# Eight PE tiles at a time for the backward 32x32 products, and 32x32 transpositions of pairs of bf16 as 4-byte elements

## The chip, the cores and the metric

One core of one Trainium2 chip. The metric is the device time of one execution in microseconds; the time before is the median of three runs. A profile is one execution, taken by the hardware profiler. In it PE is the matmul engine, PEld its weight loads, DVE the vector engine, ACT the scalar engine, POOL and SP the two engines that start most of the DMAs. L399 is line 399 of the kernel before.

## The reference

A forward pass and its gradient, on 2048 rows of 512 bf16 values. The forward pass is a layer norm, then the sum of a recurrent attention and a dense branch. What matters here is the attention: 32 heads of 128, the sequence cut into 64 segments of 32 rows, and a memory of 8 rows that each segment hands to the next.

```python
for s in range(n_seg):                                   # 64, in order
    h = jnp.concatenate([mem, xs], axis=1)               # 8 + 32 rows
    q, k, v = (jnp.einsum('btd,dhe->bhte', h, W) for W in (Wq, Wk, Wv))
    scores = jnp.where(mask, jnp.einsum('bhqe,bhke->bhqk', q, k) * scale, -1e9)
    p = softmax(scores)
    o = jnp.einsum('bhqk,bhke->bhqe', p, v)              # per head: 40x40 by 40x128
    o = jnp.einsum('bhte,hed->btd', o, Wo)
    mem = o[:, :M]
    outs.append(o[:, M:])
```

The backward pass runs the segments from the last to the first. Per head it needs dV = P^T dO, dP = dO V^T, dS from dP and P, dK = dS^T Q and dQ = dS K, then the gradient of h from dQ, dK, dV by Wq, Wk, Wv, whose first 8 rows are handed to the segment before. The gradients of the weights are summed over all rows. Eleven outputs in all.

## The kernel before, in words

The rows of a segment are kept as 32 "A" rows (8 of memory, the last 24 of the segment) that lie on the recurrence, and the first 8 rows of four segments are gathered into one "L" block of 32 rows (16 blocks in all). The L blocks hang on the recurrence only through what they share with it, and their work is used as filler. Everything is therefore 32 rows high, and a tile of 128 partitions by 8 x 128 holds 32 heads: partition 32j + r is row r, column block i is head 4i + j (j from 0 to 3, i from 0 to 7). This is the layout of qN, kN, vN, oN, gN, dN and dLN ("NAT"). The transposed layout "TR" ([128 elements of a head, i, j, 32 rows]) serves as weights (lhsT) of the PE.

Stages, each with its own planner: the dense branch with layer norm; the forward chain of 64 segments (`chain`, with `l_proj` and `l_attn` for the L blocks and `dw_unit`, the dense branch's weight gradients, as filler); turning Wv, Wk, Wq and Wo into the layouts of the backward pass (`turn`, `turn_o`); the backward chain of 64 segments (the second `chain`, with `load`, `l_pre` and `l_post`); the weight gradients of the attention (L1497 on).

Order of work: each stage adds its operations to a `_Plan` with an estimated cost per engine, the keys it reads and writes, and a priority. `run` (L101) computes ranks and writes out one fixed order; each engine then runs its own instructions in that order, and waits where a result is not there yet. PSUM has eight banks. `Stage.bank` (L350) hands them out by turn from rings per kind of use ("c" for the chain, "f" for filler, "r" for a long sum), in the order in which the program adds the operations, and the order of the plan follows from it.

One backward segment (L1300 to L1363): `proj` computes gO (32 matmuls of 32 columns of weights by 512, four column strips of the array at once, two halves), `to_T_plain` transposes it on the PE, two half runs compute dP, four DVE steps (`smax_bwd`, L1165 to L1170) give dS. `part` (L1319) is called for dV (2), dK (1) and dQ (0): `diag` (L441) multiplies per head, `sq_T` (L395) transposes the result in 32x32 blocks on DVE into dT, `dh_part` (L1174) multiplies dT by the turned weights into one long sum, dRA. Its result R_A is copied out (L1339), a small product (gm, L1349) takes the rows of the memory, and a copy (L1353) puts them into the next gO's input. So dRA, R_A, gm, gO, dP and dS form the recurrence.

`diag` computes a half (4 of the 8 column blocks i) in one PSUM bank: for each i and each of two terms, four products of 32x32 weights by 32x128, one for each j, at tile (32j, 32j) of the array: rows 32j on, columns 32j on. Four products are under way at once, on the diagonal. Its result is copied to bf16 by ACT or DVE (`evict`). The forward pass uses `diag` for O (L992 and L938), the backward for dV, dK, dQ (L1320) and dqL (L1222); `l_post` writes the same form by hand (own, L1254), and adds products of the full 128 rows to it (mm, L1265) from the loads xs and ys; dLN is stored to S_GNL and, for its first part, read back.

`sq_T`: for a half, one DVE instruction transposes 512 columns of bf16, as 16 blocks of 32x32 per strip of 32 partitions; the elements of a head are taken with a step of four (e = 4a + c), so that partition 32j + a of the result holds elements 4a + c of head 4i + j. The weights of the following product (Wo by `wo_part`, L854; turned Wq, Wk, Wv by `wtf`) are laid out to match.

## Time and profile before

| what | value |
|---|---|
| runs, us | 3017.47, 3035.89, 3026.65; median 3026.65 |
| span of the profiled execution, us | 3018.8 |
| PE, PEld, DVE, ACT, POOL busy, us | 2761.1, 1575.5, 1551.3, 967.4, 372.8 |
| DMA moved | 590 MB, 195 GB/s on average |
| mean granted clock of the PE | 0.976 |

The execution whose span this is ran its instructions over 3018.8 us; the times of the runs have the start and end of an execution around the span. Times inside the profile count from the start of the span. The stages lie at about 0 to 236 (dense branch), 236 to 1240 (forward chain), 1240 to 1276 (turning), 1276 to 2440 (backward chain), 2440 to 2490 (loads before the weight gradients) and 2490 to 3018.

```profile
PE 2761.1 (91%) x59680; PEld 1575.5 (52%) x59680; DVE 1551.3 (51%) x3367; ACT 967.4 (32%) x2013; POOL 372.8 (12%) x640
```

A group's line gives the line of the kernel, the engine, the operation, what it writes and reads, its shapes and count, then its busy time, the mean of one in ns, and the engine's idle time just before it with what ended that. "128*32 128x512" on a matmul is a weight of 128 rows by 32 columns and a moving operand of 128 by 512. A matmul's duration includes its way through the array, so many overlap; how fast they follow each other is read from the starts, in the view in order of time.

### The profile page before, as it was taken

How to read it: one execution, taken by the hardware profiler on the slowest of the kernel's cores; microseconds unless marked ns; L12 is line 12 of the kernel's file. 1: busy time of each engine (PE TensorE's matmuls, PEld its weight loads, DVE VectorE, ACT ScalarE, POOL GpSimd, SP SyncE). 2: the span in 40 equal slices, each digit the busy share in tenths (PEclk: the TensorE clock that was granted, in tenths of full speed). 3: DMA queues.
4: the chain of work that ended last, by engine and by line, in shares of the span. 5: the costliest groups of instructions: out<-in, count | busy, mean ns of one | idle time of the engine just before them, and what ended most of it. 6: DMA issues, size and time to landing. Idle time of an engine off the chain costs nothing.

```text
span 3018.8 us, 132985 instructions
## 1 busy us (share of the span) xinstructions
PE 2761.1 (91%) x59680; PEld 1575.5 (52%) x59680; DVE 1551.3 (51%) x3367; ACT 967.4 (32%) x2013; POOL 372.8 (12%) x640
## 2 busy tenths in 40 slices
PE   8998899999999999888888888888889889999998
PEld 6664555555555555655454545454555444444444
DVE  5544555555555655666555555565556522232322
ACT  4324444444454444333333333333333310000000
POOL 1111111111111111100000000000000002111111
PEclk9999999999999999899999999999999999999999
DMA  6648655556555666457777877777777689788861
GB/s 202 221 141 227 166 170 168 162 159 172 167 166 162 174 182 179 135 162 197 196 208 197 211 215 208 202 204 207 204 215 205 193 292 311 232 262 271 248 182 42
DMA packets 543946, 590.15 MB, mean 195 GB/s; under 512 B 230342, under 2 KB 344183, under 8 KB 541199
## 3 DMA queue, kind: packets, MB, share of 16 engines
q1 hardware_dynamic: 527934, 527.05, 61.2%
q0 software_dynamic: 15440, 54.61, 5.4%
q8 instruction: 466, 7.63, 1.1%
q14 instruction: 106, 0.86, 0.1%
HBM read 283.32 MB, written 262.68 MB: 181 GB/s over the span
## 4 chain that ended last, share of the span: by engine, by line
PE 64%; issue 11%; DMA 10%; DVE 9%; SPq 2%; ACT 2%; POOL 1%; DVEq 0%; ACTq 0%; POOLq 0%
PE ps_gw L1517 11%; PE ps_dRA L1181 7%; PE ps_d L451 6%; PE ps_q L415 4%; PE ps_k L415 3%; PE ps_RA L863 3%; PE ps_h L622 3%; PE ps_gO L415 3%; PE ps_dw L1073 2%; PE ps_v L415 2%; PE ps_dRL L1181 2%; PE ps_B L650 2%; SPq L361 2%; PE ps_gxb L650 2%; DMA dLN<-S_GNL 1%
## 5 line engine op out<-in xcount | busy, mean ns | idle before, releaser
L1181 PE MATMUL ps_dRA<-WA,dT 128*32 128x512 bf16 x6144 | 382.5, 388 | 13.9 <-issue 10.2
L1517 PE MATMUL ps_gw<-WA,WB 128*128 128x512 bf16 x1536 | 332.3, 379 | 0.6 <-DVE gwo L316 0.6
L415 PEld LDWEIGHTS <-PA 128*32 128x32 bf16 x8192 | 204.9, 98 | 239.2 <-DVE PA L1011 27.0
L399 DVE STREAM_TRANSPOSE dT<-dN 128x512 bf16<-128x512 bf16 x384 | 255.6, 692 | 104.9 <-ACT dN L318 103.4
L1517 PEld LDWEIGHTS <-WB 128*128 128x128 bf16 x1896 | 185.4, 98 | 225.0 <-issue 1.7
L318 ACT CAST dN<-ps_d 128x512 bf16<-128x512 f32 x357 | 199.2, 588 | 287.5 <-PE ps_d L451 270.1
L1181 PEld LDWEIGHTS <-dT 128*32 128x32 bf16 x6144 | 158.5, 98 | 175.7 <-issue 34.4
L316 DVE CAST gwo<-ps_gw 128x512 bf16<-128x512 f32 x64 | 39.7, 683 | 401.7 <-PE ps_gw L1517 268.2
L318 ACT CAST gwo<-ps_gw 128x512 bf16<-128x512 f32 x64 | 32.9, 599 | 515.4 <-PE ps_gw L1517 357.9
L1291 POOL COPY bVT<-VR 128x1024 bf16<-128x1024 bf16 x64 | 66.7, 1043 | 965.9 <-PE ps_dP L1313 917.7
L415 PE MATMUL ps_q<-WA,PA 128*32 128x512 bf16 x2048 | 159.3, 387 | 8.4 <-DVE PA L1011 8.3
L316 DVE CAST kN<-ps_k 128x512 bf16<-128x512 f32 x120 | 83.0, 691 | 160.4 <-PE ps_k L415 158.7
L451 PEld LDWEIGHTS <-PB 32*32 32x32 bf16 x8192 | 119.1, 92 | 79.3 <-issue 45.9
L415 PE MATMUL ps_k<-WA,PA 128*32 128x512 bf16 x2048 | 158.0, 385 | 0.0
L415 PE MATMUL ps_gO<-WB,PA 128*32 128x512 bf16 x2048 | 138.3, 414 | 16.8 <-DVE PA L1353 15.3
L863 PE MATMUL ps_RA<-WB,OT 128*32 128x256 bf16 x4096 | 128.3, 275 | 14.6 <-DVE OT L399 10.5
L318 ACT CAST qN<-ps_q 128x512 bf16<-128x512 f32 x124 | 72.6, 586 | 198.8 <-PE ps_q L415 183.0
L1073 PE MATMUL ps_dw<-sx,anT 128*128 128x512 bf16 x448 | 123.7, 384 | 9.3 <-DMA sx<-in_grad_out_dram 4.7
L415 PE MATMUL ps_v<-WA,PA 128*32 128x512 bf16 x2048 | 129.3, 380 | 0.0
L863 PEld LDWEIGHTS <-OT 128*32 128x32 bf16 x4096 | 103.9, 97 | 39.1 <-DVE OT L399 30.6
L844 POOL TENSOR_TENSOR P<-P,rsA 128x320 bf16<-128x320 bf16 x64 | 46.2, 722 | 534.3 <-DVE rsA L839 228.1
L1181 PE MATMUL ps_dRL<-WA,LT 128*32 128x512 bf16 x1536 | 108.9, 387 | 2.3 <-issue 1.2
(307 smaller groups left out, 4920.1 us busy)
## 6 DMA issues: line engine op xcount, KB each, us to landing
S_GN<-dN SPq DMA_DIRECT2D x192, 256.0 KB
WA<-S_GN SPq DMA_DIRECT2D x160, 256.0 KB
S_Q<-qN SPq DMA_DIRECT2D x64, 256.0 KB
S_K<-kN SPq DMA_DIRECT2D x64, 256.0 KB
S_V<-vN SPq DMA_DIRECT2D x64, 256.0 KB
S_ON<-oN SPq DMA_DIRECT2D x64, 256.0 KB
bqN<-S_Q SPq DMA_DIRECT2D x64, 256.0 KB
bkN<-S_K SPq DMA_DIRECT2D x64, 256.0 KB
```

The costliest lines, as they stand in the source:

```text
L316: nc.vector.tensor_copy(out, in_)
L318: nc.scalar.copy(out, in_)
L399: self.plan.add({"DVE": 0.70}, lambda e, x=x: nc.vector.transpose(dst[:, x, :, :], src[:, x, :].rearrange("p i (a c) -> p i c a", c=JQ)), ...
L415: nc.tensor.matmul(bk()[32 * j:32 * (j + 1), :], lhsT=win(dc), rhs=Wt(dc, c0), start=(dc == 0), stop=(dc == DC - 1), tile_position=(0, 32 ...
L451: nc.tensor.matmul(bk()[32 * j:32 * j + m, k * P:(k + 1) * P], lhsT=lf(j, i), rhs=rf(j, i), start=(k == 0 and x == 0), stop=(x == n - 1), ...
L622: nc.tensor.matmul(bk()[:, x, :], lhsT=Wt[:, dc, fc * P:(fc + 1) * P], rhs=In[:, dc, :], start=(dc == 0), stop=(dc == DC - 1), skip_group_ ...
L650: nc.tensor.matmul(bk()[:], lhsT=src[z][:, fc, rc * P:(rc + 1) * P], rhs=Wt[:, fc, :], start=(fc == 0 and first), stop=(fc == FC - 1))
L863: nc.tensor.matmul(bk()[32 * c:32 * (c + 1), :], lhsT=OTt[:, i, j, :], rhs=Wo[:, JQ * i + j, dh * DH:(dh + 1) * DH], start=(i == 0 and j < ...
L1073: nc.tensor.matmul(bks[x]()[:], lhsT=anT[x][:, c, :], rhs=sx[z][:], start=(c == 0), stop=(c == TC - 1))
L1181: nc.tensor.matmul(bk()[32 * j:32 * (j + 1), :], lhsT=XT[:, i, j, :], rhs=wtf(t, JQ * i + j), start=(first and i == 0), stop=(last and i = ...
L1291: A({"POOL": 1.0}, lambda e: nc.gpsimd.tensor_copy(VT[:, :, :, M:KA].rearrange("p i j r -> p (i j) r"), VR[:].rearrange("p i j r -> p (i j ...
L1517: nc.tensor.matmul(bks[n]()[:], lhsT=HNc[:, rc, dc * P:(dc + 1) * P], rhs=gns[y][:, hf * 512:(hf + 1) * 512], start=(y == 0), stop=(y == N ...
```

## The change: what it does

Five things go together.

**1. The products.** `cross` takes the place of `diag` in the backward pass. A half is now two values of j with all eight i, in place of all j with four i. The product of strip j and column block i goes to tile (32j, 32c), where c = i % 4: the rows are still those of strip j, but the result lands in partitions 32c on. Four column strips times two row strips (y) are addressed one after the other, eight tiles, and each of the two row strips writes its own PSUM bank (columns 0 to 255 of it). The eviction reads both banks in one instruction of 512 elements.

```diff
+        def cross_mm(self, bk, half, terms, first):
+            for s_ in range(2):
+                for x, (lf, rf, m) in enumerate(terms):
+                    for y in range(2):
+                        j = 2 * half + y
+                        for c in range(JQ):
+                            i = JQ * s_ + c
+                            nc.tensor.matmul(
+                                bk()[32 * c:32 * c + m, y, s_ * P:(s_ + 1) * P], lhsT=lf(j, i), rhs=rf(j, i),
+                                start=(first and s_ == 0 and x == 0), stop=(x == len(terms) - 1),
+                                tile_position=(32 * j, 32 * c), skip_group_check=True,
+                            )
+
+        def cross_evict(self, half, bk, dst, prio):
+            self.evict(lambda: dst[1][:, 4 * half:4 * half + 4, :].rearrange("p (y s) e -> p y (s e)", y=2), bk,
+                       lambda: bk()[:, :, 0:2 * P], [(dst[0], half)], prio, EV_F)
...
-                sg.diag("c", "d%d" % t, terms, rk, ("dN%d" % t, dN[t]), 0)
+                sg.cross("d%d" % t, terms, rk, ("dN%d" % t, dN[t]), 0, LIFT[t])
...
-            sg.diag("f", "dqL", [
+            sg.cross("dqL", [
```

`cross` plans a half as 0.115 us a term (`diag`: 0.23), and lists the half of its destination among the keys that the product writes. `l_post` does the same by hand: its own product uses `cross_mm` and now lists the loads xs and ys among what it reads; the product of 128 rows keeps its 16 matmuls a half on four column strips and writes the same two banks.

**2. The transpositions.** `sq_T`, in both passes, moves 4-byte words: 256 a half instead of 512 elements, so the element of a head that lands on partition a is e = 4a + 2c + z, with z the place in the pair. The two values of a pair stay neighbours, so a weight of 32 columns is read with a step of two elements, by `rows`.

```diff
+            words = lambda t, x: t[:].rearrange("p i j r -> p (i j r)").bitcast(F32)[:, 2 * P * x:2 * P * (x + 1)]
             for half in range(2):
-                x = slice(4 * half, 4 * half + 4)
-                self.plan.add({"DVE": 0.70}, lambda e, x=x: nc.vector.transpose(
-                    dst[:, x, :, :], src[:, x, :].rearrange("p i (a c) -> p i c a", c=JQ)),
+                self.plan.add({"DVE": 0.43}, lambda e, half=half: nc.vector.transpose(
+                    words(dst, half).rearrange("p (i c r) -> p i c r", i=4, c=2),
+                    src[:].rearrange("p i e -> p (i e)").bitcast(F32)[:, 2 * P * half:2 * P * (half + 1)]
+                    .rearrange("p (i a c) -> p i c a", i=4, c=2)),
                     [(sk, half)], [(dk, half)], prio)
+
+        def rows(self, XT, i, q):
+            return XT[:].rearrange("p i (c z) r -> p i c (z r)", c=2)[:, i, q // 2].rearrange("p (r z) -> p z r", z=2)[:, q % 2]
...
-                            nc.tensor.matmul(bk()[32 * j:32 * (j + 1), :], lhsT=XT[:, i, j, :],
-                                             rhs=wtf(t, JQ * i + j), start=(first and i == 0),
+                            nc.tensor.matmul(bk()[32 * j:32 * (j + 1), :], lhsT=sg.rows(XT, i, j),
+                                             rhs=wtf(t, i, j), start=(first and i == 0),
...
-                                    bk()[32 * c:32 * (c + 1), :], lhsT=OTt[:, i, j, :],
+                                    bk()[32 * c:32 * (c + 1), :], lhsT=sg.rows(OTt, i, j),
```

**3. The order of heads.** Strip j, column block i now holds head 16(i // 4) + 4j + i % 4. The moving operand of `proj` (`wf`) becomes one run of 512, the loads of Wo, `turn`, `wtf` and the stores of the weight gradients follow the new order; in the weight gradients the moving operand of L1517 becomes four runs of 128.

```diff
     def wf(t):
-        w = Wqkv[t].rearrange("p c (i j e) -> p c i j e", i=NI, j=JQ)
-        return lambda dc, c0: w[:, dc, c0 % HW // P:c0 % HW // P + 4, c0 // HW, :]
+        w = Wqkv[t].rearrange("p c (s j f) -> p c s j f", s=2, j=JQ)
+        return lambda dc, c0: w[:, dc, c0 % HW // 512, c0 // HW, :]
...
-    def wtf(t, h):
+    def wtf(t, i, q):
+        h = 16 * (i % 2) + JQ * (i // 2) + q
         return Wqkv[t][:, :, h * P:(h + 1) * P]
```

**4. The banks.** In the backward stage a bank is no longer handed out by turn: the planner picks, when it places the first operation on a bank, the one that has been free longest among those that the kind may use, and a kind may hold only so many at once. An operation without a free bank waits its turn in the plan. The other stages keep their rings.

```diff
-        sg = Stage(plan, {"c": (pc, 5), "r": (pc, 1), "f": (pc, 2)})
+        S3 = [("c", x) for x in range(3)]
+        sg = Stage(plan, pc, {"c": (3, S3), "f": (1, S3), "w": (3, S3), "r": (1, [("r", 0)]), "d": (2, [("d", 0), ("d", 1)]),
+                              "t": (3, [("r", 0), ("d", 0), ("d", 1)])})
...
             for o in elig:
+                got = slots(o)
+                if got is None:
+                    continue
...
                     for d in o.deps:
                         t = max(t, d.end if d.eng == e and e != "SP" else d.end + d.lat + g)
+                    for x in got:
+                        t = max(t, x[0] + g)
```

"d" is a pair of banks, two of them; so the eight banks are three shared by chain and filler, one for dRA (and the last dRL), and two pairs. `turn` in the backward stage uses "t". The factor `ACCP` and the three values of `LIFT` that the planner can weigh in are zero.

**5. The weight gradients.** The eight banks of a group are now three of "w", the one of "r" and the two pairs of "d", each pair one tile. Before the stage, three instead of four banks take early products (`mm0`).

274 lines of the change are left out of this document (154 added, 120 removed).

## The prediction

> **What bounds the kernel now.** I read the busy times by stage first, cut where the lines change: the dense branch, the forward chain of 64 segments, the turning of the weights, the backward chain of 64 segments, the loads before the weight gradients, the weight gradients. Columns: PE, weight loads, DVE, ACT, POOL, then granted clock, DMA share and GB/s.
>
> ```profile
> 0.00:236.00 236.00, 222.52 (x1654) 149.52 (x1658) 125.93 (x498) 86.49 (x213) 36.31 (x85) 1.00 0.61 194
> 236.00:1240.00 1004.00, 928.36 (x23600) 552.46 (x23589) 571.44 (x1232) 457.02 (x1021) 142.18 (x263) 0.99 0.61 171
> 1276.00:2440.00 1164.00, 1018.71 (x31361) 594.32 (x31359) 678.95 (x1349) 377.18 (x694) 91.52 (x140) 0.96 0.73 202
> 2490.00:3018.00 528.00, 520.48 (x2411) 235.69 (x2409) 146.34 (x240) 32.86 (x64) 97.31 (x144) 1.00 0.71 222
> ```
>
> PE is busy 92% of the forward chain, 88% of the backward chain and 99% of the weight gradients; DVE is at 57% and 58% in the two chains. PE bounds all three, and the backward chain leaves it 145 us idle, 2.3 us of each segment's 18.2 us. So PE time removed there should show, and DVE time only where PE waits for it. Next, the groups and the order of time inside one backward segment:
>
> ```profile
> L399 DVE STREAM_TRANSPOSE dT<-dN 128x512 bf16<-128x512 bf16 x384 | 255.6, 692 | 104.9 <-ACT dN L318 103.4
> L399 DVE STREAM_TRANSPOSE OT<-oN 128x512 bf16<-128x512 bf16 x128 | 88.9, 705 | 20.0 <-ACT oN L466 15.9
> L1330 DVE STREAM_TRANSPOSE PB<-maskA 128x256 bf16<-128x256 bf16 x64 | 27.7, 433 | 0.0
> ```
>
> ```profile
> 1611.51 0.28 PE L1313 MATMUL ps_dP<-bVT,gOT 128*32 128x40 bf16 x16
> ...
> 1617.68 0.23 PE L451 MATMUL ps_d<-bkN,PB 32*32 32x128 bf16 x4
> 1617.75 0.22 PE L451 MATMUL ps_d<-bkLN,PB 32*32 32x128 bf16 x4
> ...
> 1618.53 0.22 PE L451 MATMUL ps_d<-bkLN,PB 32*32 32x128 bf16 x4
> 1618.68 3.64 PE L1181 MATMUL ps_dRA<-WA,dT 128*32 128x512 bf16 x64
> ```
>
> The 64 products of one gradient (both halves) go four at a time: the first four start at 1617.68, the sixteenth four at 1618.53, the next work at 1618.68. That is 0.85/15 = 56.7 ns for four, 14.2 ns for a product, 1.00 us for the whole.
>
> Last, the chain of waits over the backward stage: of its 1164 us, pieces named DMA add to 134 us and pieces of SP's queue to 21 us (the sum of the 200 longest), 13% together; "issue" is 11.7%. The longest are the dLN round trip and the xs and ys loads, some 5 us each.
>
> **PE: the 32x32 products.** Twice as many tiles work at once, with the same number of products and weight loads. No row shows eight tiles in two strips of rows. Upper end of the cost: nothing gained, 14.2 ns each. Lower end: the fastest pairs of weight load and product in this trace. ps_dP starts 16 in 0.28 - 0.18 us (its own product lasts 0.18), 6.7 ns each; ps_dPL (64 from 1283.58 to 1284.07) 7.7 ns. Eight in 56.7 ns would be 7.1 ns. I take 7.2 ns, the mean of the two rows: 64 x (14.2 - 7.2) = 0.45 us a run.
> - Backward chain: 3 gradients x 64 segments + 16 dqL = 208 runs, 208 x 0.45 = 93.6 us.
> - The own product of l_post: 2 parts x 16 blocks, 32 runs of 32 products, 0.22 us each, 7.0 us.
>
> Together 101 us of PE time. The forward products (L992, L938) still go through diag and gain nothing.
>
> How much of it passes to the end: the part of the stage's chain that isn't DMA or SP's queue is 87%; if the "issue" share doesn't shrink either it is 75%. I take 80%: **-80 us** (ends -101 and 0). The recurrence doesn't stop it earlier: from gO (1608.03) to dS (1614.69) is 6.7 us, then d1 and d0 now 1.1 instead of 2.0, dRA 5.2 of which some 0.9 fits before dS, then R_A, gm and the copy 1.3, about 13 us against a segment of 18.2 - 1.6 = 16.6; the rest of a segment is the L block's filler, which PE must do anyhow.
>
> **DVE: transpositions of pairs.** 640 of them (384 + 128 + 96 + 32), about 692 ns now. They get 256 elements of 4 bytes in place of 512 of 2. The nearest rows are 256 elements of 2 bytes, 433 ns (L1330), and today's 692 if 4 bytes cost two passes. I take 433: 0.26 us saved each, 125 us of DVE in the backward stage, 42 in the forward one. Most lies beside PE's work. Backward: PE waits for dT 2.1 us and its weight loads 9.4 us; the first two of the four softmax steps sometimes queue behind a dT (one 0.70 us piece at 1627.87 in the chain). I take **-6 us** (0 to -20). Forward: before L863 PE and its loads wait 41.1 us for OT in 83 waits; each could lose up to 0.26 us, 21 us, but PE is 92% busy and only a gap that filler doesn't take counts. I take half, **-10 us** (0 to -21). If PE's cover went and DVE led, the saving would be larger, not smaller.
>
> **Weight loads with a step.** dT, LT, OT and qLT are now read with a step of two elements (dh_part, wo_part). Nothing shows a stepped load of 32 columns. The nearest are the turns: ps_Wo loads adjacent columns and ps_Wk every fourth:
>
> ```profile
> 1236.85 1.96 PE L312 MATMUL ps_Wo<-ident,WB 128*128 128x128 bf16 x32
> ...
> 1273.00 1.98 PE L312 MATMUL ps_Wk<-ident,WA 128*128 128x128 bf16 x32
> ```
>
> 32 of each in 1.96 and 1.98 us: no price. I take 0, with doubled loads as the other end (the slower rival). The moving operands change too: proj's becomes one run of 512, L1517's four runs of 128. ps_gO reads four runs of 128 (32 products in 1.91 us) as do ps_dRA's, at the same 54 ns; 0.
>
> **PSUM banks.** The backward chain had five banks c, two f, one r. Now c and f share three, r keeps one, and two double banks take dN, dqL and dL. gO takes two of the three, and gOT's halves need gO's eviction anyway, dP needs gOT's; so two would do, and the third covers the one f that may be open. A d0 product needs d1's half evicted: d1 0.5 us, then 0.6 of ACT, during which 16 products of dRA (0.87 us) run as they do at 1616.70. If that cover is missing in every segment it costs one eviction, 64 x 0.6 = 38 us; a gain is possible as well, since a bank is now chosen when it is free and not by turn. I take 0 (+38 to -10). The eviction reads two banks in one instruction of 512 elements: ACT 588 ns today; ACT has 377 of 1164 us busy, so even a quarter more hides.
>
> **Waits and the queues.** The own product of dL now follows xs and ys in the order: PE's next work there needs the same loads directly afterwards, so a late load holds the same instruction stream. No DMA is added, moved or resized; SP and POOL issue what they did. The transposition's reader and writer are the same tiles.
>
> **Weight gradients.** Two banks form one tile, so the seventh product of a group waits for both evictions. Around 2664 the last DVE eviction ends at 2666.94 and the seventh product is due at about 2666.88: some 0.15 us x 15 groups, **+2 us**. Early products drop from four banks to three per load; 1.3 us move behind the 5 us loads that PE waits for there anyway.
>
> **Sum** on the profiled execution: -80 - 6 - 10 + 2 = -94, span 3018.8 to 2925. The span is 7.9 us below the median of the runs (3026.65) and within their 3017.47 to 3035.89; I subtract from the median: **2933 us**.
>
> **Rivals.**
> 1. *The gain goes into DMA.* The dLN round trip and the xs and ys loads keep their 5 us, and with DMA at 0.73 now they would be at 0.78 in a shorter stage. For: up to 6.4 us in one wait. Against: that chain is some 20 us a block of 73. If only 40% passes: -40 - 6 - 10 + 2 = -54, 2973 us. Chance 0.13.
> 2. *The eight tiles don't overlap*, so the change doesn't do what it says: products stay at 14.2 ns. For it, no row with two strips of rows on one column strip; against it, ps_dP's 6.7 ns shows that the issue isn't the limit. Then -6 - 10 + 2 = -14, 3013 us. Chance 0.11. The Trainium skill, "TensorE: Matmul & The Clock Gate", section "Wait — 56ns, not 53.3ns?", states that start-to-start never drops below about 25 ns; by that rule this rival would be certain, but the trace has 14.2 and 6.7 ns, so the rule can't hold over several tiles. The same page, Part 3, gives 10.6x for 16 packed tiles, which speaks for the overlap; no run here shows it.
> 3. *Slower: stepped weight loads take twice as long.* Place: wo_part, where 64 pairs take 1.97 us, 27 ns each once the tail of 0.27 is off, the tightest use of these tiles. If a pair took 54 ns, (4096 + 1024) x 27 ns = 138 us in a stage with PE at 92%; dh_part, at 54 ns a pair, would just hide it. -94 + 138 = +44, 3071 us. It turns the sign from 94/5120 = 18 ns more a pair. Against it are the turns above. Chance 0.08, with what else would make it slower.
>
> **The numbers.** The forecast has 0.68, with its own range from everything passing (-101 - 20 - 21 - 10 + 2 = -150, 2877) to the bank stalls (-56, 2971). The range 2880 to 2995 takes in rival 1 and leaves out rivals 2 and 3, 0.19. Half a per cent, 15 us, is about what a measurement of this kernel tells from no change. Faster by more: 0.68 + 0.13 + half of rival 2 = 0.86; within: the most of its other half, 0.05; slower: 0.09.
>
> **What would show it.** ps_d: 64 products in about 0.55 us and not 1.0, PE's busy time on ps_d from 226 to some 120 us. L399's successor near 433 ns. ps_RA and ps_RL still 64 in 1.97 us. The backward stage near 1078 us, the forward one near 994, the weight gradients near 530. The forecast is wrong if ps_d's starts stay at 14 ns a product, if ps_RA's spacing grows, or if PE's idle time in the backward stage grows from 145 to over 190 us.

## The result

| | before | after | ratio, 95% interval |
|---|---|---|---|
| runs, us (median) | 3025.10 | 3075.16 | 1.0166 [1.0134, 1.0197] |
| span of the profiled execution, us | 3018.8 | 3070.4 | |
| mean granted clock of the PE | 0.976 | 0.959 | |

The change made the kernel 50 us slower, by 1.7%; the forecast was 2933 us. One of the four runs of after took 6963.30 us, at a granted clock of 1.0; the ratio leaves it out, and its cause is not known. The busy times by stage, cut at the same places as before, the last one later since the kernel ends later (columns as there: PE, weight loads, DVE, ACT, POOL, clock, DMA share, GB/s):

```profile
0.00:236.00 236.00, 221.27 (x1659) 149.45 (x1686) 126.45 (x499) 86.96 (x214) 37.07 (x84) 0.99 0.62 186
236.00:1240.00 1004.00, 897.02 (x22863) 539.04 (x22976) 525.93 (x1227) 426.39 (x937) 133.41 (x247) 0.96 0.63 168
1276.00:2440.00 1164.00, 969.26 (x30481) 496.14 (x30479) 596.39 (x1392) 339.86 (x613) 92.87 (x143) 0.93 0.73 196
2490.00:3060.00 570.00, 563.30 (x2692) 253.48 (x2698) 147.59 (x242) 33.81 (x64) 93.46 (x137) 1.00 0.74 232
```

In the backward window PE is busy 49 us less than before and DVE 83 us less, as was wanted, and yet fewer matmuls fit into it (30481, before 31361), at a clock of 0.93 instead of 0.96. The stages no longer lie where they lay, so the next table is cut at events of the trace instead: the first ps_qL (the first projection of the forward chain; an expectation below calls it ps_q), the first and the last ps_RA, the gO of the second and of the last backward segment, the end. Its rows are worked out from the matmuls' starts, in us; "before, again" is a second profile of the kernel before, from an experiment below, to show how far such pieces repeat.

| piece | before | before, again | after | after less before |
|---|---|---|---|---|
| start to first ps_qL | 230.3 | 230.4 | 228.7 | -1.6 |
| to the first ps_RA: start of the forward chain | 18.1 | 18.7 | 51.6 | +33.5 |
| to the last ps_RA: forward chain | 987.4 | 983.5 | 980.2 | -7.2 |
| to the second gO: turning, start of the backward chain | 66.5 | 66.4 | 76.2 | +9.7 |
| to the last gO: 62 backward segments | 1120.4 | 1124.7 | 1133.4 | +13.0 |
| to the end: last segment, weight gradients | 596.2 | 595.7 | 600.3 | +4.1 |

Two things want a cause: 33 us lost once, where the forward chain starts, and 62 segments that gained nothing.

**The instructions themselves came out as forecast.** The transposition groups of after (a line's groups: busy, mean ns, idle before):

```profile
L438 DVE STREAM_TRANSPOSE dT<-dN 128x256 f32<-128x256 f32 x384 | 162.1, 434 | 109.5 <-ACT dN L357 104.3
...
L438 DVE STREAM_TRANSPOSE OT<-oN 128x256 f32<-128x256 f32 x128 | 55.6, 441 | 23.3 <-ACT oN L538 19.5
```

434 and 441 ns, where 433 was forecast. PE in order of time in one backward segment of after:

```profile
1657.76 0.25 PE L503 MATMUL ps_d<-gON,bP 32*32 32x128 bf16 x8
1657.83 0.24 PE L503 MATMUL ps_d<-gLN,bPLL 32*8 32x128 bf16 x8
1657.88 0.24 PE L503 MATMUL ps_d<-gON,bP 32*32 32x128 bf16 x8
...
1661.80 0.23 PE L503 MATMUL ps_d<-bqN,maskA 32*32 32x128 bf16 x5
1663.44 0.23 PE L503 MATMUL ps_d<-bqN,maskA 32*32 32x128 bf16 x3 [1.41 <-issue]
...
1667.34 0.21 PE L503 MATMUL ps_d<-bkN,PB 32*32 32x128 bf16 x1
1668.83 0.24 PE L503 MATMUL ps_d<-bkN,PB 32*32 32x128 bf16 x7 [1.28 <-issue]
...
1670.46 3.42 PE L1257 MATMUL ps_dRA<-WA,dT 128*32 128x512 bf16 x32 [0.67 <-DVE dT L438]
```

Eight products start within 57 ns (1657.76, 1657.83, 1657.88), 7.1 ns each, so eight tiles do work at once. But then PE stops in the middle of a run of eight, after the fifth, for 1.41 us, and again after the first of eight for 1.28 us. The products just before and after read the same tiles, so no operand was missing; the profile names no releaser ("issue"). From the first stop to the second PE issued 128 pairs of weight load and product. The long sum behind it runs at half rate: 32 matmuls in 3.42 us, where 32 between the two stops took 1.91. Each of after's waits of this kind beside its counterpart of before (the queue's waits: total us, times, longest):

```profile
PEld L503 <- issue: 135.8, 209, 3.3
...
PEld L1257 <- issue: 94.0, 249, 3.4
```

```profile
PEld L451 <- issue: 74.5, 113, 4.4
...
PEld L1181 <- issue: 42.4, 98, 2.0
```

**The start of the forward chain.** The longest pieces of the chain of waits there, and PE's view of the same time:

```profile
230.50 26.81 DMA out_dram<-PB
...
260.04 35.57 DMA S_QL<-lN
```

```profile
248.75 1.89 PE L459 MATMUL ps_vL<-WA,PB 128*32 128x512 bf16 x15 [9.62 <-issue]
...
279.07 1.89 PE L459 MATMUL ps_qL<-WA,PB 128*32 128x512 bf16 x15 [17.69 <-issue]
280.34 2.33 PE L937 MATMUL ps_RA<-WB,OT 128*32 128x256 bf16 x32
285.88 1.25 PE L937 MATMUL ps_RA<-WB,OT 128*32 128x256 bf16 x16 [3.21 <-DMA WB<-in_A_Wo_dram]
288.50 0.62 PE L937 MATMUL ps_RA<-WB,OT 128*32 128x256 bf16 x8 [1.37 <-DMA WB<-in_A_Wo_dram]
295.46 0.62 PE L937 MATMUL ps_RA<-WB,OT 128*32 128x256 bf16 x8 [6.34 <-DMA WB<-in_A_Wo_dram]
```

The first sum over Wo (ps_RA, 64 products) waits for its eighths one by one, and smaller transfers that share the time take 27 and 36 us. The 64th product starts 66.9 us after the first ps_qL; before it was 21.9 us, in both profiles. The two long stops before this sum, 9.62 and 17.69 us, have no releaser and lie exactly 128 weight loads apart, as the two stops in the backward segment lie 128 pairs apart. A transfer of instructions had landed 1.6 us before the first of them ended, but 20 us before the second did, so what held the second stays open.

### The profile page after: what moved, and what is told of

It is laid out like the page before. It is cut to its first block, busy times and chain, and to the rows that moved or that the text cites. A ratio compares the mean times of both kernels' runs of the same rounds, so it can differ in the third digit from the quotient of the medians.

```text
span 3070.4 us, 132905 instructions
## 1 busy us (share of the span) xinstructions
PE 2724.2 (89%) x59519; PEld 1479.4 (48%) x59680; DVE 1443.1 (47%) x3461; ACT 918.2 (30%) x1886; POOL 373.4 (12%) x640
## 4 chain that ended last, share of the span: by engine, by line
PE 58%; issue 22%; DMA 7%; DVE 6%; ACT 3%; POOL 2%; SPq 1%; ACTq 0%; POOLq 0%; DVEq 0%
PE ps_dRA L1257 11%; PE ps_d L503 4%; PE ps_q L459 4%; PE ps_gO L459 4%; PE ps_k L459 3%; PE ps_RA L937 3%; PE ps_h L696 3%; PE ps_v L459 3%; PE ps_dRL L1257 2%; PE ps_o L523 2%; PE ps_dw L1147 2%; PE ps_gxb L724 2%; PE ps_B L724 2%; POOL out_dram L1598 1%; PE ps_gOT L351 1%
## 5 line engine op out<-in xcount | busy, mean ns | idle before, releaser
L1257 PE MATMUL ps_dRA<-WA,dT 128*32 128x512 bf16 x6144 | 430.8, 421 | 52.0 <-DVE dT L438 26.0
L357 ACT CAST dN<-ps_d 128x512 bf16<-128x512 f32 x302 | 172.9, 586 | 340.3 <-PE ps_d L503 303.6
L438 DVE STREAM_TRANSPOSE dT<-dN 128x256 f32<-128x256 f32 x384 | 162.1, 434 | 109.5 <-ACT dN L357 104.3
L459 PE MATMUL ps_gO<-WB,PA 128*32 128x512 bf16 x2048 | 125.2, 384 | 10.1 <-DVE PA L1422 6.7
L1147 PE MATMUL ps_dw<-sx,anT 128*128 128x512 bf16 x323 | 104.6, 387 | 14.2 <-DMA sx<-in_grad_out_dram 9.1
L355 DVE COPY R_A<-ps_dRA 128x256 f32<-128x256 f32 x63 | 26.7, 424 | 174.2 <-ACT R_A L357 164.4
```

Source lines behind the costliest of these rows:

```text
L355: nc.vector.tensor_copy(out, in_)
L357: nc.scalar.copy(out, in_)
L438: self.plan.add({"DVE": 0.43}, lambda e, half=half: nc.vector.transpose(words(dst, half).rearrange("p (i c r) -> p i c r", i=4, c=2), src[ ...
L459: nc.tensor.matmul(bk()[32 * j:32 * (j + 1), :], lhsT=win(dc), rhs=Wt(dc, c0), start=(dc == 0), stop=(dc == DC - 1), tile_position=(0, 32 ...
L1147: nc.tensor.matmul(bks[x]()[:], lhsT=anT[x][:, c, :], rhs=sx[z][:], start=(c == 0), stop=(c == TC - 1))
L1257: nc.tensor.matmul(bk()[32 * j:32 * (j + 1), :], lhsT=sg.rows(XT, i, j), rhs=wtf(t, i, j), start=(first and i == 0), stop=(last and i == N ...
```

## Experiments

Two theories stood at the beginning. For the start: the load of Wo has become slow, against the planner's new order. For the segments: PE's instructions arrive too slowly for the quicker products, against the shared banks and the new order. The runs went over several chips, so times are compared by their ratio to the kernel before, run on the same chip.

### How far one profile repeats

> The kernel before once more, unchanged, to see how far its stages repeat from one profile to the next: forward chain (first to last ps_RA) 987 us and backward chain (first to last gO) 1148 us in the first profile. If the backward chain's stalls come at fixed places of a fixed instruction stream, both repeat within 5 us; if they depend on when transfers land, they differ by 10 to 20 us, and differences of that size between two kernels' single profiles mean nothing.

The second column of the table above: the forward chain 3.9 us apart, the segments 4.3 us. After's own instruction order, run again in the experiment on Wo, took 1119.7 us for the 62 segments, 13.7 us less than after's 1133.4. So the segments of before and after (1120 to 1125 and 1120 to 1133) can't be told apart: they neither gained nor lost, within some 14 us. The 33.5 and the 9.7 us are outside that scatter.

### The load of Wo, by strips

The new order of heads puts four heads that lie four apart into one column block, and the load followed it. This run makes each transfer one strip of all four blocks of a half, four neighbouring heads:

```diff
-            sg.dma(lambda i=i: Wo[:, JQ * i:JQ * (i + 1), :].rearrange("p c d -> p (c d)"),
-                   lambda i=i: A_Wo.rearrange("(s j x) (a c) d -> s x j a (c d)", s=2, j=JQ, c=JQ)[i // JQ, i % JQ],
+            s_, j_ = i // JQ, i % JQ
+            sg.dma(lambda s_=s_, j_=j_: Wo[32 * j_:32 * (j_ + 1), JQ * JQ * s_:JQ * JQ * (s_ + 1), :].rearrange("p (x c) d -> p x (c d)", c=JQ),
+                   lambda s_=s_, j_=j_: A_Wo[16 * s_ + JQ * j_:16 * s_ + JQ * (j_ + 1)].rearrange("x (a c) d -> a x (c d)", c=JQ),
```

> The changed kernel, with Wo loaded by other eight transfers: one for four neighbouring heads (32 partitions, runs of 4 KB) instead of one for four heads that lie four apart (128 partitions). The same bytes land in the same places. If the slow load of Wo (37.1 us a transfer after the change, 11.7 before) is what holds the start of the forward chain, the time from the first ps_q to the first ps_RA falls from 51.6 back to 18 to 22 us and the whole from 3075 to 3040 to 3047 us. Rival: the new order of the forward stage is what holds the start, and the load only shares the time; then the start keeps some 50 us and the whole stays within 5 us of 3075.

Measured: ratio 1.0009 [0.9993, 1.0025], level with before, 0.0157 or 47 us less than after. The first ps_RA comes 17.0 us after the first ps_qL, and the forward chain behind it takes 967.6 us. The DMA view of 215 to 300 us (queue: packets, MB, share of the 16 engines; and the load: KB each, median us to landing), in before, after and this run:

```profile
q0 software_dynamic: 1632, 6.03, 21.8%
...
WB<-in_A_Wo_dram POOLq DMA_DIRECT2D x8, 512.0 KB, 11.7
```

```profile
q0 software_dynamic: 4704, 6.04, 63.6%
...
WB<-in_A_Wo_dram POOLq DMA_DIRECT2D x8, 512.0 KB, 37.1
```

```profile
q0 software_dynamic: 1632, 6.03, 29.3%
...
WB<-in_A_Wo_dram POOLq DMA_DIRECT2D x8, 512.0 KB, 11.5
```

The same 6 MB went out with 4704 packets in place of 1632. The data are 1472 packets of 4096 bytes in after as by strips; the 384 more for each of the eight loads are packets of 4 bytes. A data packet took 551 ns on average in after, 269 by strips and 200 before, and the load held the engines more than twice as long; everything that shared them was late. Whether the small packets slow the others, or the source in four pieces does, is not shown.

By strips the 64th product of the first sum over Wo starts 27.9 us after the first ps_qL, 39 us earlier than in after. The other 8 us lie behind it (956.7 us to the last ps_RA, in after 964.9) and are no more than profiles of this order scatter by. In the next two experiments, which keep after's load, the first ps_RA comes after 34.0 and 36.1 us and not 51.6, yet the 64th product after 66.1 and 65.9: the end of the load sets it, whatever PE waited for on the way. Behind that sum they take 955.8 and 955.0 us to the last ps_RA. The first theory holds. And behind that sum the forward chain of after's order gained on before, which took 983.6 and 980.3 us there.

### The products issued strip of rows by strip of rows

After, with only the order of the loops in `cross_mm` changed, so that a strip of rows is finished before the next:

```diff
-            for s_ in range(2):
-                for x, (lf, rf, m) in enumerate(terms):
-                    for y in range(2):
-                        j = 2 * half + y
+            for y in range(2):
+                j = 2 * half + y
+                for s_ in range(2):
+                    for x, (lf, rf, m) in enumerate(terms):
```

> The changed kernel, with the eight-tile products issued strip of rows by strip of rows, so that four tiles work at a time again (some 14 ns a product); banks, order of the plan, transpositions and loads stay as after the change. If the products' gain is taken back by PE waiting for its own instructions (mid-run stalls of 1.2 to 1.4 us, 61 us of them before the change and 101 after) and by the half clock that follows (75 us before, 124 after), the slower products cost almost nothing: stalls go back to some 60 us, the whole stays within 25 us of 3075. Rival: the gain of 80 us is real and lost elsewhere, to the three shared banks or the new order; then the whole rises to some 3150 us, with stalls as they are.

Measured: ratio 1.0173 [1.0150, 1.0196], after's own being 1.0166; the 62 segments took 1128.6 us. The edit did less than was meant. From the first to the last start of a half of 32 products it is 10.2 ns a product on average (8.1 in the median), against 8.0 in after and 13.9 before, halves that a stop interrupts left out: most halves still overlap the two strips. PE's busy time on ps_d is 193 us, after 167 and before 226. So this run puts back 26 us of PE time, not the whole gain, and these 26 us cost nothing that can be measured. For them the rival, that the gain is real and lost to the banks or the order, is out; for the rest of the gain this run doesn't tell. From the starts of the matmuls and the landings of the instruction transfers (queue q8 of the trace), for these 62 segments:

| us | before, twice | after | Wo by strips | strip of rows by strip |
|---|---|---|---|---|
| 62 segments | 1120.4, 1124.7 | 1133.4 | 1119.7 | 1128.6 |
| PE busy | 977, 968 | 943 | 943 | 969 |
| idle inside a run, ending 1.0 to 2.3 us after an instruction transfer landed | 66, 80 | 109 | 91 | 80 |
| other idle | 78, 77 | 81 | 86 | 80 |
| time at half clock | 85, 55 | 140 | 137 | 154 |

The 26 us that this run adds to PE's busy time come out of its waits for instructions (109 to 80 us).

PE's busy time fell by 30 us from before to after, and not by the forecast's 101. The products gave less: ps_d is at 167 us and not at the 120 of the forecast. And time at half clock counts as busy. It grew by some 70 us, and most of it lies in the long sum ps_dRA, which the change left as it was. The groups before and after:

```profile
L1181 PE MATMUL ps_dRA<-WA,dT 128*32 128x512 bf16 x6144 | 382.5, 388 | 13.9 <-issue 10.2
L1257 PE MATMUL ps_dRA<-WA,dT 128*32 128x512 bf16 x6144 | 430.8, 421 | 52.0 <-DVE dT L438 26.0
```

In the 62 segments PE spends 396 us on ps_dRA, 103 of them at half clock; before it was 348 and 346 us, with 22 and 16 at half clock. Counting time at half clock as half of it, PE's work in the 62 segments fell from 940 us (mean of before's two) to 878, in after and by strips alike. Of these 62 us the half clock took back 32, and idle time 27 (Wo by strips) to 40 us (after), most of it behind instruction transfers. That is the whole gain: it went in about equal parts to two takers.

### What a long run of products takes

After, with four runs of 1024 products in turn, on eight tiles and on four, ahead of the backward chain:

```diff
+                for k in range(n):
+                    y, c = (k // 4) % 2, k % 4
+                    r = c if diag else y
+                    nc.tensor.matmul(lrb()[32 * c:32 * (c + 1), y, 0:P], lhsT=q_(Wqkv[2], r)[:, 0, 32 * (k % 16):32 * (k % 16) + 32],
+                                     rhs=q_(Wqkv[2], r)[:, 1, P * (k % 16):P * (k % 16) + P], start=True, stop=True,
+                                     tile_position=(32 * r, 32 * c), skip_group_check=True)
```

> The changed kernel with four long runs of 1024 products of 32x32 weights by 32x128 added ahead of the backward chain, on data that is there already: two in the order of eight tiles, two in the order of four on the diagonal, in turn. They write two PSUM tiles that nothing needs; outputs as before. If PE's instructions arrive more slowly than the eight tiles use them (a block of 128 pairs of load and product takes some 1.1 us to transfer and PE starts again 1.2 to 1.6 us after it landed at the latest), a run of eight tiles shows a gap at every block and takes 9 to 13 us, 9 to 13 ns a product, with half the starts in between at 7 ns; the order of four takes 14.5 us without gaps. Rival: the stalls in the chain are waits for something else; then a run of eight tiles takes 7.3 us without gaps.

PE in order of time in this run; the first five lines are eight tiles, the last three four tiles:

```profile
1304.61 2.03 PE L1456 MATMUL ps_long<-WA 32*32 32x128 bf16 x220
1309.07 1.91 PE L1456 MATMUL ps_long<-WA 32*32 32x128 bf16 x128 [2.43 <-issue]
1312.54 1.91 PE L1456 MATMUL ps_long<-WA 32*32 32x128 bf16 x128 [1.56 <-issue]
1316.01 1.91 PE L1456 MATMUL ps_long<-WA 32*32 32x128 bf16 x128 [1.56 <-issue]
1319.76 1.91 PE L1456 MATMUL ps_long<-WA 32*32 32x128 bf16 x128 [1.84 <-issue]
...
1407.44 1.97 PE L1456 MATMUL ps_long<-WA 32*32 32x128 bf16 x128 [0.31 <-issue]
1410.91 1.96 PE L1456 MATMUL ps_long<-WA 32*32 32x128 bf16 x128 [1.51 <-issue]
1414.38 1.97 PE L1456 MATMUL ps_long<-WA 32*32 32x128 bf16 x128 [1.51 <-issue]
```

The first 220 pairs go in 2.03 us. From there on PE gets exactly 128 pairs and then nothing, and a new 128 start every 3.47 to 4.02 us, on eight tiles as on four: 26 to 29 ns a pair in the mean of each run, whatever the pair takes. This is more than the 9 to 13 ns expected, and the expectation that four tiles would run without gaps was wrong too. The queue's line for 1304 to 1402 us, and the busy times of a stretch in it:

```profile
q8 instruction: 27, 0.44, 1.8%
```

```profile
1305.00:1340.00 35.00, 20.42 (x1347) 18.63 (x1334) 1.84 (x3) 0.32 (x1) 0.00 (x0) 0.61 0.02 5
```

27 transfers of 16 KB in 98 us, one every 3.6, while nothing else moves (DMA share 0.02), so it isn't contention. The whole kernel before has 59680 pairs and 466 such transfers, 128 pairs each. A transfer takes 1.05 to 1.11 us in the median of each trace, but in no trace of this case does the next start less than 3.2 us after its start. And the clock falls to 0.61 in these 35 us, with PE idle 42% of the time. Over the whole runs it is the eight tiles that lose it: they spend 23.3 of 27.1 us and 26.2 of 28.3 us at half clock, the runs on four tiles 7.4 of 29.1 and 8.0 of 29.4. A block of 128 then takes 1.91 us on eight tiles at half clock, as long as the 1.97 on four at full clock.

The Trainium skill, "TensorE: Matmul & The Clock Gate", section "Wait — 56ns, not 53.3ns?", has a floor of about 25 ns from start to start for small matmuls. The prediction set it aside because of bursts at 7 and 14 ns, and bursts do run at that; but the long run's mean, 27 ns, is close to it, though here it is the instructions' transfers that set it. The Trainium skill, same page, "Part 1: The HAM clock gate", has the clock halve after an idle window of about 3.4 us; here the half-rate stretches in the segments are multiples of 3.41 us, but each of the 33 that begin in after's 62 segments follows a window with PE idle for only 0.8 to 3.2 of the 3.41 us.

### Pairs added and left out

The second term of dV and dK (the memory rows) left out, with Wo by strips; those gradients lack that part:

```diff
             part(2, [(lambda j, i: q_(Pt[z], j)[:, i, M:KA], lambda j, i: q_(gN, j)[:, i, :], 32),
-                     (lambda j, i: q_(PLL[p], j)[:, i, c0:c0 + M], lambda j, i: q_(gLN[p], j)[:, i, :], M)],
...
             part(1, [(lambda j, i: q_(dS, j)[:, i, M:KA], lambda j, i: q_(qN, j)[:, i, :], 32),
-                     (lambda j, i: q_(dSL[p], j)[:, i, c0:c0 + M], lambda j, i: q_(qLN[p], j)[:, i, :], M)],
```

> The changed kernel with Wo loaded strip by strip, and without the memory rows' products in dV and dK (the second term of d2 and d1): 64 x 2 x 32 = 4096 pairs of load and product fewer in the backward chain, so that those gradients lack the part of the L block's rows. By the time that the products take on eight tiles (7.1 ns each) that is worth 4096 x 7.1 = 29 us. By the instruction supply (3.5 us for 128 pairs when it is what PE waits for, 27 ns a pair) it is worth up to 4096 x 27.3 = 112 us, and at least 58 us (the 14.2 ns a product that four tiles took). So 2988 us beside 3017 for the one, 2905 to 2960 for the other.

Ratio 0.9783 [0.9752, 0.9814]: 68 us less than with Wo by strips alone (1.0009, of 3025), 17 ns a pair; not the products' 7.1. But the planner takes a product's cost from its number of terms, so the order moved too. The next four hold that cost (for the two lists above, 2 terms whatever their length), and leave the pairs out or issue the second term twice, in the changed kernel with Wo by strips and in the one before:

> The changed kernel with Wo loaded strip by strip, and the second term of dV and dK (the memory rows) multiplied and added twice: 4096 pairs of load and product more in the backward chain, so those gradients hold that part twice; planned costs held, so the order is that of the kernel with Wo by strips (ratio 1.001). By the products' time on eight tiles 4096 x 7.1 = 29 us, ratio 1.010 to 1.012; by the instruction supply 60 to 112 us, ratio 1.020 to 1.038.

> The kernel before with the same 4096 pairs more, planned costs held, so its own order. By the products' time on four tiles 4096 x 14.2 = 58 us, ratio 1.019; twice what the changed kernel pays. By the instruction supply the same 60 to 112 us as in the changed kernel, ratio 1.020 to 1.037, since a pair is fetched as slowly whatever its tiles.

> The changed kernel with Wo loaded strip by strip, without the second term of dV and dK (those gradients lack the L block's rows): 4096 pairs fewer, planned costs held. By the products' time -29 us, ratio 0.991 to 0.993; by the instruction supply -60 us or more, ratio 0.981 or below. The run that left the same pairs out with the planner's order changed as well had 0.978.

> The kernel before without the second term of dV and dK: 4096 pairs fewer, planned costs held, its own order. By the products' time on four tiles -58 us, ratio 0.981; by the instruction supply the same as the changed kernel loses, -60 to -112 us, ratio 0.963 to 0.980.

| 4096 pairs | ratio, 95% interval | against | us (of 3026) | ns a pair |
|---|---|---|---|---|
| more, after with Wo by strips | 1.0415 [1.0397, 1.0432] | 1.0009 | +123 | 30 |
| more, before | 1.0366 [1.0342, 1.0389] | 1 | +111 | 27 |
| fewer, after with Wo by strips | 0.9732 [0.9705, 0.9758] | 1.0009 | -84 | 20 |
| fewer, before | 0.9804 [0.9779, 0.9830] | 1 | -59 | 14 |

More pairs cost 27 to 30 ns each in both kernels, the 27 ns of the long run, though products start 14.2 ns apart in the kernel before and 7.1 in the changed one. Idle time behind an instruction transfer grows in the 62 segments from 91 to 155 us in the changed kernel and from 73 (mean of two) to 139 in the kernel before. Fewer pairs give 20 ns each in the changed kernel, and in the kernel before 14 ns, just their own time: there the supply was near its limit and not beyond it.

What a pair's price is made of, in the 62 segments, with time at half clock counted half as above:

| us | whole | PE's work | half clock | idle |
|---|---|---|---|---|
| more, after with Wo by strips | +123 | +35 | +33 | +55 |
| more, before | +105 | +62 | -3 | +46 |
| fewer, after with Wo by strips | -76 | -36 | -23 | -16 |
| fewer, before | -64 | -58 | +4 | -10 |

In the kernel before, the half clock plays no part, and pairs added there cost their own time and then 46 us of waiting: the supply is shown as a limit that this chain meets. In the changed kernel it is one of two; a quarter to a third of what pairs cost or give there is the half clock, so its 20 and 30 ns are not the supply's price alone. Neither slope is the same in both directions, so the supply is not the whole bound of the chain: some 240 blocks in the backward chain at 3.5 us would be 840 of its 1150 us.

### The transpositions, and the planner's order

The kernel before with `sq_T` and `rows` of the change and nothing else, the planner told 0.43 us:

```diff
-                            nc.tensor.matmul(bk()[32 * j:32 * (j + 1), :], lhsT=XT[:, i, j, :],
+                            nc.tensor.matmul(bk()[32 * j:32 * (j + 1), :], lhsT=sg.rows(XT, i, j),
...
-                self.plan.add({"DVE": 0.70}, lambda e, x=x: nc.vector.transpose(
-                    dst[:, x, :, :], src[:, x, :].rearrange("p i (a c) -> p i c a", c=JQ)),
+                self.plan.add({"DVE": 0.43}, lambda e, half=half: nc.vector.transpose(
```

> The kernel before, with nothing but the transpositions changed: pairs of bf16 as 4-byte elements, and the weights of the following products read with a step of two. Products, heads, banks and loads as before. If the pairs give what the prediction said, 6 us in the backward chain and 10 us in the forward one, the whole is 3005 to 3013 us. Rival: without the faster products PE covers DVE in both chains and nothing shows, 3020 to 3028 us; a cost of the stepped loads would show above 3030.

Ratio 1.0005 [0.9989, 1.0022]. Nothing shows in the whole, but the forward chain took 956.5 us (before 983 to 987) and the 62 segments 1143.0 (1120 to 1125). The same with the planner still told 0.70:

> The kernel before with the transpositions of pairs and the stepped weights, but the planner is still told 0.70 us for a transposition, so every engine keeps the order of before and only the instructions are quicker. The variant whose planner was told 0.43 came out even with before, its forward chain 31 us shorter and its backward chain 22 us longer. If the backward loss was the new order, this one keeps the forward gain without it: 2985 to 3000 us beside 3014 to 3025 of before. Rival: quicker transpositions only bring PE sooner to its instruction supply (a block of 128 pairs no faster than 3.3 us); then nothing shows, within 8 us of before.

Ratio 0.9993 [0.9973, 1.0014], forward chain 984.7, segments 1131.1. In the order of before the quicker instruction is worth nothing that can be measured, as the rival said; whether PE covers it or waits for its instructions instead is not separated. And the other half, the order of 0.43 with the old 692 ns instruction:

```diff
-                self.plan.add({"DVE": 0.70}, lambda e, x=x: nc.vector.transpose(
+                self.plan.add({"DVE": 0.43}, lambda e, x=x: nc.vector.transpose(
```

> The kernel before with its own transpositions of 2-byte elements (692 ns), and only the planner told 0.43 us for them: the order of the pairs' variant with the old instruction. If the 31 us of the forward chain came from the order, it keeps 20 to 31 of them and the backward chain's loss as well, ratio 0.998 to 1.003. Rival: the quicker instruction is what makes that order good; then the forward chain is back at 980 us or above and the whole is slower than before, ratio 1.005 or more.

Ratio 1.0048 [1.0030, 1.0065]: forward chain 972.4, segments 1161.1. It falls between the two expectations. In the forward chain order and instruction give about half each, as far as single profiles tell; in the backward one that order loses 40 us with the slow instruction and some 20 with the quick one. So the kernel before with the pairs and each stage's better order, 0.43 forward and 0.70 backward:

```diff
-                self.plan.add({"DVE": 0.43}, lambda e, half=half: nc.vector.transpose(
+                self.plan.add({"DVE": 0.70 if getattr(self, "slow", False) else 0.43}, lambda e, half=half: nc.vector.transpose(
...
         sg = Stage(plan, {"c": (pc, 5), "r": (pc, 1), "f": (pc, 2)})
+        sg.slow = True
```

> The kernel before (products on four tiles, its heads, banks and loads) with the transpositions of pairs, and the planner told 0.43 us for them in the forward stage and 0.70 us in the backward one. With 0.43 in both, the forward chain was 31 us shorter and the backward one 22 us longer; with 0.70 in both, neither moved. If order is what counts, each stage by itself, this one keeps the forward gain without the backward loss: ratio 0.988 to 0.993, better than both kernels. Rival: the two differences were chance, or hang together; ratio 0.998 to 1.002.

Ratio 0.9917 [0.9879, 0.9955], 2999.58 us where before took 3031.71 on that chip: forward chain 962.4, segments 1122.9. It beats both kernels, by 0.8%, with an order of the forward stage that the quicker transposition makes possible.

Could another order have saved the eight tiles? Three runs on the changed kernel with Wo by strips: the planner told 0.43 us for a term of a half of products (the supply's price), told the costs of before in the backward stage (0.23 and 0.70), or given no preference for staying with one shape of matmul there.

```diff
-                self.plan.add(pe(0.115 * n, "d"), mm, rkeys(half), [bk, (dst[0], half)], prio, lift=lift)
+                self.plan.add(pe(0.43 * n, "d"), mm, rkeys(half), [bk, (dst[0], half)], prio, lift=lift)
```

> The changed kernel with Wo loaded strip by strip, and the planner told 0.43 us for each term of a half of products (16 pairs at 27 ns, what the supply of instructions allows) in place of 0.115. Same instructions, another order. If the order that the planner finds with a false cost leaves PE without work where the instructions come late, the backward chain gains 10 to 30 us: 2985 to 3007 us beside 3017. Rival: the supply is a total (some 240 blocks) that no order changes; then within 8 us of 3017.

> The changed kernel with Wo loaded strip by strip; in the backward stage alone the planner is told the costs of before (0.23 us for a term of a half of products instead of 0.115, 0.70 us for a transposition instead of 0.43). Banks, tiles and instructions as after the change. If the order that follows from the short costs puts products together faster than PE's instructions arrive, the order of the longer costs gains 10 to 25 us on 1.001 of before: ratio 0.993 to 0.998. Rival: the freed time goes into the supply of instructions in any order; ratio 0.999 to 1.003.

```diff
-KEEP = 2.0
+KEEP = 0.0
```

> The changed kernel with Wo loaded strip by strip, and the planner's preference for staying with one shape of matmul in the backward stage taken from 2.0 us to 0, so that products and the long sums mix more. If bursts of products are what PE's instruction supply can't follow, the mixing lessens the stalls behind a fetched block (91 us in segments 2 to 63) to 50 to 70 and the whole to a ratio of 0.985 to 0.995. Rival: changing shape costs PE more than the stalls, or the recurrence is delayed by filler; ratio above 1.005.

All three missed. Ratios 1.0300 [1.0271, 1.0329], 1.0272 [1.0240, 1.0303] and 1.0046 [1.0026, 1.0066]; the segments took 1214.3, 1223.1 and 1152.7 us. Idle behind an instruction transfer was 76, 83 and 104 us (91 with Wo by strips alone), so the third did not lessen it. In the first two PE waits between runs instead, 132 and 116 us (69 with Wo by strips alone), and spends 317 and 295 us at half clock (137). With these banks an order can cost 100 us, and after's was the best of the four tried. No run keeps the eight tiles and gives the banks back, so what the banks do is not separated.

## Why the prediction was wrong

- **What bounds the kernel.** "PE time removed there should show" is the sentence that failed. PE was busy 88% of the backward stage, but its own instruction supply stood close behind: 59680 pairs at 27 ns are 1610 us in all, and in bursts it was already waited for (66 to 80 us in the segments of before). And the clock did not stay: time at half clock rose from 55 and 85 us to some 140. Of the 62 us of work that left the 62 segments, 27 to 40 became idle time and 32 went to the half clock; nothing that shows passed to the end. The prediction read "issue" as a share of the chain (11.7%) that might not shrink; it did not ask what issues. On the pages of the whole execution it rose from 11% to 22% of the chain.
- **The products, -80 us.** The mechanism came as forecast in bursts (57 ns for eight, 7.1 ns each), but the term of 101 us was too large as well: on ps_d PE was busy 226 us and is 167, not 120. What passes on is nothing. The two rows that gave 7.2 ns, ps_dP and ps_dPL, are bursts of 16 and 64, short enough to run from instructions that are there already; stops in the middle of a run came more often after the change. PE's idle time in the window 1276 to 2440 rose from 145 to 195 us, past the 190 that the prediction gave as its own refutation.
- **The transpositions, -6 and -10 us.** The price was right (434 ns for 433), the worth in the given order is nothing, within 6 us. In the forward chain some 15 to 29 us came in another way (behind the first sum over Wo 955 to 965 us in four runs with after's forward order, 980 to 984 before): the planner makes another order of a shorter cost, and in that order the quick instruction counts, as the kernel before with pairs shows. The prediction did not think of the order, so that the sign of its -10 us came out is luck.
- **Weight loads with a step, 0.** Right: 64 products of ps_RA start within 1.66 us in the median, before as after, and the kernel before with pairs was not slower. Rival 3 named the right sign by a mechanism that did not occur.
- **Rival 1**, that the gain goes into DMA, did not come: DMA's share of the chain of waits fell from 10% to 7% (pages of the whole execution).
- **Rival 2**, that eight tiles don't overlap, was wrong in the mechanism, though its -14 us is nearest to what the changed kernel with Wo by strips does.
- **Waits and queues: "No DMA is added, moved or resized".** This was wrong, and the dearest single step. The loads of Wo keep their number and bytes, but read other heads, and 47 us hang on that. The diff shows the line; its cost was set at nothing without asking how the source lies in memory.
- **Banks, 0 (+38 to -10).** Nothing contradicts it, and nothing shows it: the 62 segments as a whole gained and lost nothing, and no run changes the banks alone. Some 10 us went at the start of the backward chain (66.5 to 76.2 us, and 76.4 with Wo by strips), where the turns use the shared banks; which of banks and order does it wasn't tried.
- **Weight gradients, +2.** +4.1 in after's profile, +1.7 with Wo by strips.
- **The half clock** was in no part of the prediction. It is 55 to 85 us of before's segments and 137 to 154 in the three kernels with after's order; the kernel before has 75 with the pairs in its old order and 106 in the new one. So it moves with the order. The long runs show that it also goes with quicker products: on the same supply of instructions the eight tiles spent 86 to 93% of their time at half clock, the four tiles 25 to 27%. That the instruction stalls bring it about is not shown: with 4096 pairs more the kernel before stalls 139 us and has only 65 at half clock, the changed one 155 and 229. The cause stays open.

## What to carry to other kernels

Before making small matmuls quicker, count them: where PE waits for its instructions, a pair of load and matmul costs some 27 ns here however little PE does for it. In the backward chain quicker products were worth nothing, and leaving out 4096 of them 59 to 84 us. Look at the clock beside the busy time: a long sum at half clock looks like work. When an order of heads or blocks changes, look at every transfer that follows it, and count its packets and what one of them takes, not its bytes. And where a planner writes the order, a new cost changes two things, the instruction and the order; try them apart, and stage by stage.

## What the hardware showed

- PE's instructions arrive in transfers of 16 KB, 128 pairs of weight load and matmul each. A transfer takes 1.05 to 1.11 us, the next starts 3.2 us after its start at the earliest, and in a long run 128 pairs start every 3.47 to 4.02 us with the DMA engines otherwise idle. Some 220 pairs can run ahead of it.
- Eight 32x32 tiles in two strips of rows that write two PSUM banks start 57 ns apart per eight, in bursts.
- A transposition of 256 4-byte elements takes 434 ns, as one of 256 2-byte elements; 512 2-byte elements take 692.
- A load of 512 KB that reads four heads lying four apart, as one transfer onto 128 partitions, lands in 37.1 us; four neighbouring heads onto 32 partitions in 11.5. The first has 384 packets of 4 bytes more, and its 4096-byte packets took 551 ns on average, those of the second 269.
- Runs of 1024 products on eight tiles, waiting for instructions, spent 23.3 of 27.1 and 26.2 of 28.3 us at half clock; on four tiles 7.4 of 29.1 and 8.0 of 29.4.
